# A dense layer with Mish on one core: the first load of x in two halves, one weight slab on another queue, one filler matmul fewer

## The chip, the core and the metric

The kernel runs on one core of a Trainium2 chip. The core's engines run side by side and meet at semaphores: TensorE (matmuls into the accumulators, PSUM), VectorE, ScalarE, GpSimd, and SyncE, which here only issues DMAs. A DMA is issued from an engine's queue (here SyncE's or ScalarE's); its data is moved by the core's 16 DMA engines, and a semaphore tells of its landing. The metric is the time of one execution in microseconds (us) on the device.

## The reference

All inputs are bf16. With x of 2048 tokens by 512, w1 of 512 by 1792 and w2 of 1792 by 512:

```python
h = jnp.einsum("bsd,df->bsf", x, w1) + b1
sp = jnp.log1p(jnp.exp(-jnp.abs(h))) + jnp.where(h > 0, h, jnp.zeros_like(h))
act = h * jnp.tanh(sp)
return jnp.einsum("bsf,fd->bsd", act, w2)
```

`act` is the Mish function of `h`. Two matrix products with a function between them; nearly all arithmetic is TensorE's.

## The kernel before, in words

The tokens stand in 16 tiles of 128 and in four blocks of 512 (`BLOCKS`). D = 512 is cut into four slices of 128, called k 0 to 3; F = 1792 into 14 slices f. For each block the first product (`mm1_step`, line 189) takes, for each f, four matmuls over k, with a slice of w1 as the weights and x transposed (`xT`, feature by token) as the moving operand, into one of the PSUM banks. ScalarE applies Mish with b1 as the bias (line 172) into `a_sb`. The second product (`mm2_step`, line 212) takes 14 matmuls over f for a tile of 128 tokens, then ScalarE copies the result out and SyncE stores it. A small part of tile 3 (448 columns of one f) is computed on VectorE instead (line 233), along the whole run.

The change sits in the prologue, the stretch before the first real matmul. Its parts, in order:

- Lines 113 and 6: TensorE runs fillers, matmuls on constants whose results nobody reads: five of 512 columns and two of 256 (`WARM`). They are there so that the array is at work before data has come. `t_fill[2]` is the third of them.
- Lines 115 to 118: ScalarE loads its function table, waits for a memset of VectorE (`t_bz`), and issues two loads of w1: k 0 and k 2, each for the first 8 slices f (`OPEN`), 128 partitions of 2 KB, 256 KB in all.
- Line 119: SyncE issues the load of x tiles 0 and 1 in their natural order, 128 partitions of 2 KB (`x_nat`; partition p holds the tokens 2p and 2p+1), 256 KB. Line 120: it issues k 1 of w1, 256 KB. Line 121: it waits for the third filler. Line 122: it issues a transposing load of tiles 2 and 3 straight into `xT`; then come k 3, b1, the rest of w1 (slices 8 to 13), and w2. All of these stand in SyncE's queue one behind the other.
- Lines 137 to 139: GpSimd and VectorE make an identity matrix.
- `transpose_x` (line 145): TensorE waits for `x_nat` and the identity (line 147), then turns tiles 0 and 1 with 16 small matmuls against the identity, each on 64 partitions (line 156), in four groups; after each group VectorE or ScalarE copies the result from PSUM into `xT` (line 164).
- Line 293 on: the first block in an order written out by hand: k 0 for tile 0 and f 0 to 3, then for tile 1, then k 0 for f 4 to 7 on both tiles, then k 1 and k 2 on both tiles, then k 0 to 2 on tiles 2 and 3, then k 3 on all four. Each of these matmuls waits for its own slab of w1 (`t_w1`) and for its own part of `xT` (`t_cp`).

All loads issue through `load` (line 91), which gives each its own semaphore; in the profile they all stand at line 93.

Of the kernel before, what the change touches and what calls it, by code (L numbers as in the profile page):

```python
# [4 lines left out]

P = 128
SQ = 32
WARM = (512,) * 5 + (256,) * 2
BLOCKS = (512, 512, 512, 512)
LATE = 3  # L10
VF = 1
# [26 lines left out]
def bass_standalone__dense_activation_mish__prompt_kernel(  # L38
# [16 lines left out]
    x2, out2 = x[0], out[0]  # L55
# [3 lines left out]
    OPEN = 8  # L59
    N0 = BLOCKS[0] // P  # L60

    with ExitStack() as es:
        def sb(name, shape, t):
            return es.enter_context(nc.sbuf_tensor(name, shape, t))

        x_nat = sb("x_nat", [P, 2, D], BF)
# [15 lines left out]
        def sem(name):  # L82
            return es.enter_context(nc.semaphore(name))

        sp = Stream(nc.sync, None)
        pe = Stream(nc.tensor, sem("c_pe"))
# [4 lines left out]
        def load(q, dst, src, name, transpose=False):  # L91
            s = sem(name)
            (q.eng.dma_start_transpose if transpose else q.eng.dma_start)(dst, src).then_inc(s, 16)
            return (s, 16)

        def load_w1(q, ks, a, b):
            return load(q, w1_sb[:, ks, a * P:b * P], w1v[:, ks, a * P:b * P], "s_w1_%d_%d" % (ks.start, a))
# [6 lines left out]
        def load_part(q, k0, k1, a, b):  # L104
            t = load_w1(q, slice(k0, k1), a, b)
            for f in range(a, b):
                for k in range(k0, k1):
                    t_w1[k, f] = t
# [3 lines left out]
        c_m = nc.const_aps.tensor(1.0, [P, 512], BF)  # L112
        t_fill = [pe.mark(nc.tensor.matmul(ps[:, 7, 0:n], c_w, c_m[:, 0:n], start=True, stop=True)) for n in WARM]  # L113

        act.eng.preload_act_table(ACT.Mish)  # L115
        act.wait(t_bz)
        for k in (0, 2):
            load_part(act, k, k + 1, 0, OPEN)
        t_xn = load(sp, x_nat[:, :, :], x2[0:2 * P, :].rearrange("(p j) d -> p j d", p=P), "s_xn")
        load_part(sp, 1, 2, 0, OPEN)  # L120
        sp.wait(t_fill[2])
        t_x23 = load(sp, xT[:, :, 2 * P:4 * P], x2[2 * P:4 * P, :], "s_x23", True)
        load_part(sp, 3, 4, 0, OPEN)
# [15 lines left out]
        t_id = dve.mark(nc.vector.tensor_scalar(ident[:, :], diff[:, :], 0, None, ALU.is_equal))  # L139
# [4 lines left out]

        def transpose_x():

            pe.wait(t_xn, t_id)
            H = P // 2
            for b0, eng, js, ks in ((0, dve, (0,), (0,)), (2, act, (1,), (0,)), (4, dve, (0, 1), (1,)), (6, act, (0, 1), (2, 3))):
                m = len(js)  # L150
                for i, k in enumerate(ks):
                    for n, j in enumerate(js):
                        lo = (i * m + n) * H
                        for h in (0, 1):
                            g = slice(h * H, (h + 1) * H)
                            mm = nc.tensor.matmul(ps[:, b0 + h, lo:lo + H], x_nat[g, j, k * P:(k + 1) * P], ident[g, g],  # L156
                                                  start=True, stop=True)
                eng.wait(pe.mark(mm))
                for i, k in enumerate(ks):
                    dst = xT[:, k, js[0] * P:(js[-1] + 1) * P].rearrange("p (j h t) -> p j h t", j=m, h=2)  # L160
                    src = ps[:, b0:b0 + 2, i * m * H:(i + 1) * m * H].rearrange("p h (j t) -> p j h t", j=m)
                    if m == 1:
                        dst, src = dst[:, 0], src[:, 0]
                    t = eng.mark(nc.vector.tensor_copy(dst, src) if eng is dve else act.eng.activation(dst, src, ACT.Copy))  # L164
                    for j in js:
                        t_cp[j, k] = t
                free[b0] = free[b0 + 1] = [t]
# [118 lines left out]
        def spread_b1():  # L286
# [4 lines left out]
            return dve.mark(nc.vector.tensor_copy(b1_sb[:, :], b1_T[:, 0:FT]))  # L291

        transpose_x()
        t_b1c = spread_b1()
        first(range(4), (0,), (0,))
# [74 lines left out]
```

## Time and profile before

| what | value |
|---|---|
| median of 3 runs | 104.3 us (104.25 to 104.85) |
| profiled execution | 104.08 us |
| its span, first to last instruction of the program | 102.7 us |
| granted TensorE clock over the span | 1.000 |
| DMA traffic over the span | 24.76 MB, mean 241 GB/s |

How the profile is read: PE is TensorE's matmuls, PEld its weight loads, DVE VectorE, ACT ScalarE, POOL GpSimd, SP SyncE; a trailing q (SPq, ACTq) is the engine's queue, where DMAs are issued. A row of the timeline gives the start and the length in us, the engine, the line of the code, the operation, what it writes and reads, and how many were merged; in brackets stand the idle time of the engine before it and what ended that. A matmul's length in the trace includes the passage through the array, so lengths overlap; the distance between two starts tells the pace. The time to landing of a DMA counts from the start of its issue. The chain that ended last is followed back from the last instruction, at each step to whatever released it. In the view by windows, each engine has its busy time and count, and the last three columns are the granted clock, the mean busy share of the DMA engines, and the rate in GB/s of the packets that started in the window.

### The profile page before, as it was taken

The page shows a single profiled execution, that of the slowest core. Times are in us where ns is not written, and L with a number is a line of the kernel's source. Part 1 is how long each engine was busy: PE and PEld are TensorE (multiplying, and loading weights), DVE is VectorE, ACT ScalarE, POOL GpSimd, SP SyncE. Part 2 cuts the span into 40 slices and gives each one's busy share as a digit, 9 for nine tenths or more (in the row PEclk, how much of TensorE's full clock was granted, in tenths as well). Part 3 has the DMA queues.
Part 4 walks back from the last instruction along what each step waited for, and adds up shares of the span by engine and source line. Part 5 has one row for each costly group of instructions (what it writes and reads, how often), then busy time and mean ns, then how long its engine had stood idle before and what let it go on. Part 6 is the DMA issues. An engine that isn't in the chain of part 4 may idle for free.

```text
span 102.7 us, 1352 instructions
## 1 busy us (share of the span) xinstructions
PE 99.6 (97%) x518; PEld 48.7 (47%) x527; DVE 80.0 (78%) x142; ACT 48.2 (47%) x75; POOL 0.4 (0%) x5
## 2 busy tenths in 40 slices
PE   6999999999999999999999999999999999999993
PEld 2587444444444444444444444444444444444472
DVE  1203000695979599999999999999999999999972
ACT  4301999220777781022588872222277776210210
POOL 1000000000000000000000000000000000000000
PEclk9999999999999999999999999999999999999999
DMA  2999999999799999789496838497857839111103
GB/s 62 371 281 359 366 262 360 255 330 228 303 273 228 378 429 373 201 325 297 184 320 172 338 73 364 105 347 224 293 153 306 284 124 341 67 57 51 51 0 102
DMA packets 15442, 24.76 MB, mean 241 GB/s; under 512 B 8396, under 2 KB 12748, under 8 KB 13388
## 3 DMA queue, kind: packets, MB, share of 16 engines
q1 hardware_dynamic: 15004, 24.12, 72.8%
q10 hardware_dynamic: 432, 0.56, 1.5%
q8 instruction: 4, 0.07, 0.2%
q14 instruction: 2, 0.02, 0.1%
HBM read 20.71 MB, written 2.10 MB: 222 GB/s over the span
## 4 chain that ended last, share of the span: by engine, by line
PE 97%; issue 1%; DVE 0%
PE ps L189 47%; PE ps L212 47%; PE ps L113 3%; PE ps L156 1%; DVE o_sb L271 0%
## 5 line engine op out<-in xcount | busy, mean ns | idle before, releaser
L233 DVE SCALAR_TENSOR_TENSOR acc<-w_bc,a_tok,acc 128x448 f32<-128x448 bf16 x126 | 75.4, 681 | 3.0 <-DMA w_bc<-in_w_dram 3.0
L189 PE MATMUL ps<-xT,w_sb 128*128 128x512 bf16 (+2 forms) x247 | 48.8, 355 | 0.4
L212 PE MATMUL ps<-w_sb,a_sb 128*128 128x512 bf16 (+3 forms) x248 | 48.7, 354 | 0.2
L172 ACT ACTIVATE a_sb<-ps,b_sb 128x512 bf16<-128x512 f32 x56 | 37.2, 698 | 12.8 <-PE ps L189 7.6
L189 PEld LDWEIGHTS ps<-xT,w_sb 128*128 128x128 bf16 x252 | 24.2, 98 | 24.2 <-DVE xT L164 0.3
L212 PEld LDWEIGHTS ps<-w_sb,a_sb 128*128 128x128 bf16 x252 | 23.1, 98 | 25.5 <-issue 0.3
L247 ACT ACTIVATE o_sb<-ps 128x512 bf16<-128x512 f32 x14 | 8.4, 598 | 32.7 <-PE ps L212 32.7
L230 DVE TENSOR_SCALAR acc<-w_bc,a_tok 128x448 f32<-128x448 bf16 x2 | 0.8, 450 | 10.4 <-DMA w_bc<-in_w_dram 10.4
L113 PE MATMUL ps<-const-bfloat16-1.0 128*128 128x512 bf16 (+1 forms) x7 | 2.7, 563 | 0.8 <-PEq L355 0.8
L289 DVE STREAM_TRANSPOSE b_T<-b_nat 32x32 bf16<-32x32 bf16 x4 | 0.8, 202 | 3.3 <-DMA b_nat<-in_b_dram 3.2
L164 DVE CAST xT<-ps 128x128 bf16<-128x128 f32 (+1 forms) x2 | 0.6, 352 | 2.4 <-PE ps L156 2.4
L271 ACT ACTIVATE o_sb<-ps 128x320 bf16<-128x320 f32 x1 | 0.4, 438 | 4.1 <-PE ps L212 4.1
L113 PEld LDWEIGHTS ps<-const-bfloat16-1.0 128*128 128x128 bf16 x7 | 0.9, 135 | 2.1 <-issue 2.1
L164 ACT ACTIVATE xT<-ps 128x256 bf16<-128x256 f32 (+1 forms) x3 | 0.9, 347 | 1.8 <-PE ps L156 1.7
L115 ACT ACT_TABLE_LOAD x1 | 1.3, 1283 | 0.7 <-PEq L355 0.7
L271 DVE CAST o_sb<-ps 128x128 bf16<-128x128 f32 (+1 forms) x2 | 0.5, 258 | 1.1 <-PE ps L212 1.0
L110 DVE MEMSET b_nat<- 32x64 uint32 x1 | 0.1, 112 | 0.8 <-PEq L355 0.8
L243 DVE TENSOR_TENSOR o_sb<-ps,acc 128x448 bf16<-128x448 f32 x1 | 0.6, 625 | 0.1
L241 DVE TENSOR_TENSOR acc<-acc 128x448 f32<-128x448 f32 x1 | 0.6, 624 | 0.0
L156 PEld LDWEIGHTS ps<-ident,x_nat 64*128 64x128 bf16 x16 | 0.5, 123 | 0.4 <-DMA x_nat<-in_x_dram 0.4
L156 PE MATMUL ps<-ident,x_nat 64*128 64x64 bf16 x16 | 0.6, 237 | 0.0
L139 DVE TENSOR_SCALAR ident<-diff 128x128 bf16<-128x128 int32 x1 | 0.2, 227 | 0.2 <-POOL diff L137 0.2
(7 smaller groups left out, 1.0 us busy)
## 6 DMA issues: line engine op xcount, KB each, us to landing
w_bc<-in_w_dram SPq DMA_DIRECT2D x16, 1024.0 KB, 4.9
out_dram<-o_sb SPq DMA_DIRECT2D x15, 128.0 KB, 2.3
w_sb<-in_w_dram SPq DMA_DIRECT2D x1, 1792.0 KB, 11.0
w_sb<-in_w_dram SPq DMA_DIRECT2D x1, 768.0 KB, 5.8
w_sb<-in_w_dram ACTq DMA_DIRECT2D x2, 256.0 KB, 3.7
w_sb<-in_w_dram SPq DMA_DIRECT2D x2, 256.0 KB, 3.6
x_nat<-in_x_dram SPq DMA_DIRECT2D x1, 256.0 KB, 2.6
out_dram<-o_sb SPq DMA_DIRECT2D x1, 80.0 KB, 1.6
```

The lines of the kernel that those rows point to most:

```text
L113: t_fill = [pe.mark(nc.tensor.matmul(ps[:, 7, 0:n], c_w, c_m[:, 0:n], start=True, stop=True)) for n in WARM]
L115: act.eng.preload_act_table(ACT.Mish)
L156: mm = nc.tensor.matmul(ps[:, b0 + h, lo:lo + H], x_nat[g, j, k * P:(k + 1) * P], ident[g, g], start=True, stop=True)
L164: t = eng.mark(nc.vector.tensor_copy(dst, src) if eng is dve else act.eng.activation(dst, src, ACT.Copy))
L172: t = act.mark(act.eng.activation(a_sb[:, f, starts[s]:starts[s + 1]], ps[:, bank, 0:n], ACT.Mish, bias=b1_sb[:, f:f + 1]))
L189: return nc.tensor.matmul(ps[:, bank, lo:hi], w1_sb[:, k, f * P:(f + 1) * P], xT[:, k, starts[s] + lo:starts[s] + hi], start=first, stop=( ...
L212: return nc.tensor.matmul(ps[:, bank, c:hi - lo], a_sb[:, f, i * P:(i + 1) * P], w2_sb[:, f, lo + c:hi], start=(f == 0), stop=(f == FT - 1))
L230: t = dve.mark(nc.vector.tensor_scalar(o, w, col, None, ALU.mult))
L233: t = dve.mark(nc.vector.scalar_tensor_tensor(o, w, col, o, ALU.mult, ALU.add))
L247: t = [act.mark(act.eng.activation(dst, src, ACT.Copy))]
L271: t = eng.mark(nc.vector.tensor_copy(dst, src) if eng is dve else act.eng.activation(dst, src, ACT.Copy))
L289: t = dve.mark(nc.vector.transpose(b1_T[j * SQ:(j + 1) * SQ, :], b1_nat[:, j * SQ:(j + 1) * SQ]))
```

## The change

Four edits in the prologue, no other:

- `WARM` has one filler of 256 columns instead of two.
- ScalarE issues k 0, k 1 and k 2 of w1, in this order, instead of k 0 and k 2.
- SyncE issues `x_nat` as two loads of 64 partitions each (128 KB each, partitions 0 to 63 and 64 to 127), each with its own semaphore, and no longer issues k 1. The second half stands in SyncE's queue where k 1 stood, ahead of the wait for the third filler.
- The transposes wait for the identity and for both halves.

```diff
-WARM = (512,) * 5 + (256,) * 2
+WARM = (512,) * 5 + (256,)
...
-        for k in (0, 2):
+        for k in (0, 1, 2):
             load_part(act, k, k + 1, 0, OPEN)
-        t_xn = load(sp, x_nat[:, :, :], x2[0:2 * P, :].rearrange("(p j) d -> p j d", p=P), "s_xn")
-        load_part(sp, 1, 2, 0, OPEN)
+        xv = x2[0:2 * P, :].rearrange("(p j) d -> p j d", p=P)
+        t_xn = [load(sp, x_nat[h:h + P // 2, :, :], xv[h:h + P // 2, :, :], "s_xn%d" % h) for h in (0, P // 2)]
         sp.wait(t_fill[2])
         t_x23 = load(sp, xT[:, :, 2 * P:4 * P], x2[2 * P:4 * P, :], "s_x23", True)
...
-            pe.wait(t_xn, t_id)
+            pe.wait(t_id, *t_xn)
```

## The prediction, written before the changed kernel ran

> **What bounds the kernel now.** I read the page's engine totals first, then the chain of waits that ended last in order of time, then the timeline of the first 5 us, the DMA rate in windows, and the landings of the first loads. The page:
>
> ```profile
> PE 99.6 (97%) x518; PEld 48.7 (47%) x527; DVE 80.0 (78%) x142; ACT 48.2 (47%) x75; POOL 0.4 (0%) x5
> ...
> PE 97%; issue 1%; DVE 0%
> ```
>
> TensorE is both the busiest engine and nearly the whole chain. The chain in order of time shows where it could be shorter (columns: start, length, what):
>
> ```profile
> 0.73 0.04 issue
> 0.77 2.71 PE ps L113 x7
> 3.49 0.54 PE ps L156 x16
> 4.03 0.13 issue
> 4.16 5.42 PE ps L189 x52
> 9.58 0.05 issue
> 9.64 6.85 PE ps L189 x31
> ```
>
> From 4.16 us on it is one stream of matmuls without a gap worth naming, and nothing in this change touches how many there are. What the change can move is the prologue: fillers (L113), the 16 transposes (L156), their copies, and the first real matmul at 4.16 us. If that matmul moves by d and the loads behind it keep up, the end moves by d. So the question is what ended the wait ahead of the transposes and what came between them and 4.16:
>
> ```profile
> 0.74 0.40 SPq L93 DMA_DIRECT2D x_nat<-in_x_dram  x1
> ...
> 0.95 0.86 ACTq L93 DMA_DIRECT2D w_sb<-in_w_dram  x2
> ...
> 1.20 0.41 SPq L93 DMA_DIRECT2D w_sb<-in_w_dram  x1
> ...
> 2.24 1.30 SPq L93 DMA_TRANSPOSE xT<-in_x_dram  x1
> ...
> 3.42 0.45 PEld L156 LDWEIGHTS ps<-ident,x_nat 64*128 64x128 bf16 x16 [0.41 <-DMA x_nat<-in_x_dram]
> ...
> 3.70 0.62 DVE L164 CAST xT<-ps 128x128 bf16<-128x128 f32 x2 [2.38 <-PE ps L156]
> 3.75 0.98 ACT L164 ACTIVATE xT<-ps 128x128 bf16<-128x128 f32 x3 [1.73 <-PE ps L156]
> 4.13 11.87 PEld L189 LDWEIGHTS ps<-xT,w_sb 128*128 128x128 bf16 x84 [0.26 <-DVE xT L164]
> ```
>
> The transposes start at 3.42, when x_nat lands, and the first matmul follows the first copy. From landing to matmul is a fixed path: 4.16 - 3.42 = 0.74 us. The last two fillers, each in its own timeline row:
>
> ```profile
> 2.86 0.42 PE L113 MATMUL ps<-const-bfloat16-1.0 128*128 128x256 bf16 x1
> ```
> ```profile
> 3.07 0.42 PE L113 MATMUL ps<-const-bfloat16-1.0 128*128 128x256 bf16 x1
> ```
>
> They start 0.21 us apart, so the array is free again at about 3.07 + 0.21 = 3.28. The landing, not the filler, is the last to end, by about 0.1 us.
>
> **The change, part by part.** The heart of it is the order in which the DMA engines serve the first loads. Data rates (columns after the engines: granted clock, DMA share, GB/s):
>
> ```profile
> 1.20:1.60 0.40, 0.40 (x3) 0.12 (x2) 0.12 (x1) 0.40 (x1) 0.00 (x0) 1.00 0.00 0
> ```
> ```profile
> 1.60:2.00 0.40, 0.40 (x2) 0.13 (x1) 0.00 (x0) 0.40 (x1) 0.00 (x0) 1.00 0.96 113
> 2.00:2.40 0.40, 0.40 (x2) 0.15 (x1) 0.00 (x0) 0.02 (x1) 0.00 (x0) 1.00 0.49 128
> 2.40:2.80 0.40, 0.40 (x2) 0.15 (x1) 0.00 (x0) 0.00 (x0) 0.00 (x0) 1.00 1.02 384
> 2.80:3.20 0.40, 0.40 (x3) 0.15 (x1) 0.00 (x0) 0.00 (x0) 0.00 (x0) 1.00 1.02 374
> 3.20:3.60 0.40, 0.40 (x10) 0.18 (x10) 0.00 (x0) 0.00 (x0) 0.00 (x0) 1.00 1.09 410
> 3.60:4.00 0.40, 0.40 (x16) 0.27 (x11) 0.30 (x2) 0.25 (x1) 0.00 (x0) 1.00 1.00 384
> 4.00:4.40 0.40, 0.27 (x7) 0.27 (x6) 0.32 (x1) 0.36 (x3) 0.00 (x0) 1.00 1.07 389
> ```
>
> Added up, 96 KB (of 1000 bytes) have started by 2.4 us, 250 by 2.8, 400 by 3.2, 564 by 3.6, 717 by 4.0 and 873 by 4.4. Each of the first loads is 262 KB. So one load's worth is reached at 2.83 us, two at 3.50, three at 4.18. Now the landings, from the view by tile; x_nat, then k 0 of w1 alone, then k 0 and k 1 together (so the larger is k 1), then k 1 and k 2 (the larger is k 2), then the transposed load of tiles 2-3:
>
> ```profile
> DMA to landing us min/median/max: 2.6/2.6/2.6
> ```
> ```profile
> DMA to landing us min/median/max: 3.1/3.1/3.1
> ```
> ```profile
> DMA to landing us min/median/max: 3.1/3.3/3.5
> ```
> ```profile
> DMA to landing us min/median/max: 3.5/3.9/4.3
> ```
> ```profile
> DMA to landing us min/median/max: 4.3/4.3/4.3
> ```
>
> With the issue times above: x_nat at 0.74 + 2.6 = 3.34, k 0 at 0.95 + 3.1 = 4.05, k 1 at 1.20 + 3.5 = 4.70. Each is 0.51 to 0.55 us behind the moment when the bytes up to and including it had started. That is service in the order of issue, whole loads one behind the other, whichever ring they came from. Two alternatives do not fit: had SyncE's ring been emptied first, k 1 (same ring as x_nat, issued at 1.20, and x_nat's own data began about 1 us behind its issue) would have come ahead of k 0; had the rings been shared evenly, x_nat and k 0 would have landed closer together.
>
> The terms:
>
> 1. *x_nat split.* The first half goes out at 0.74, the second when SyncE is through with the first: in k 1's place, 1.20. Between them ScalarE issues k 0 at 0.95. By the order just read the engines then serve half (131 KB), k 0 (262 KB), half (131 KB). The second half is complete when two loads' worth has moved: 3.50 instead of 2.83, so x is in 0.67 us later, at 3.34 + 0.67 = 4.01. Bounds: below, the second half follows the first directly, 0 (a gain is bounded under the rivals); above, k 1 slips in as well, 4.18 - 2.83 = 1.35. I take 0.67, since k 1 is issued behind k 0 on ScalarE, at 0.95 + 0.43 = 1.38 by the two-issue row, behind 1.20.
> 2. *The path behind it* keeps its length of 0.74 plus the 0.08 from landing to the first weight load: the first matmul moves from 4.16 to 4.83. k 0 lands earlier than before, so it does not bind.
> 3. *One filler fewer*: -0.21 us of TensorE, worth nothing, because the landing is what the transposes wait for. Its cover is the landing at 4.01; the array stands idle from 3.07 to about 4.09 instead of 3.28 to 3.42.
> 4. *k 1 and k 2 of w1.* Issuing: one more DMA on ScalarE, 0.43, ending near 2.24; its first copy is at 3.75, so nothing. k 1 stays third in the order, 4.70. From 4.16 the stream takes 5.42 us for 12288 columns (8 matmuls of 128, 44 of 256), 0.44 ns a column; k 1 is wanted 2048 columns on, 0.90 us, k 2 4096 columns on, 1.81, tiles 2-3 6144 columns on, 2.71. Before, that was 5.06, 5.97 and 6.87 against landings of 4.70, 1.38 + 4.3 = 5.68, and 2.24 + 4.3 = 6.54: margins of 0.3. With a stream from 4.83 all margins grow by 0.67. k 2 is now issued 0.43 later, and could at worst let the transposed load pass it; even 0.9 us for that fits the margin. Zero, between 0 and 0.3.
> 5. *SyncE behind the halves*: the transposed load waits for the third filler, as before, and goes out at 2.24, later than the second half's issue ends (1.20 + 0.41). Nothing moves behind it.
> 6. *One more wait on TensorE* ahead of the transposes: both counts are there when the second half lands; the chain's smallest issue gaps are 0.04 to 0.05, so 0 to 0.05, and I take 0.
>
> Sum: +0.67 us. The profiled execution took 104.08 us for a span of 102.7; it becomes 103.4 and 104.75. The median of the runs shown is 0.22 above the profiled execution, so **105.0 us**.
>
> **The rivals.**
>
> *No queueing: nothing happens (0.17).* If the second half is served directly behind the first, x lands at 3.34 as before, k 0 still at 4.05, and the time is 104.3. For it: both halves are on one ring, and the order of issue was read from whole loads of equal size only. Against it: k 0's issue is 0.25 us ahead of the second half's. The Trainium skill, "DMA: Bandwidth & Descriptors", Rules for kernel authors, says of two transfers to disjoint partition halves "Don't bother", as both use the same 16 DMA engines and only serialize; by that alone the split would be this case, 104.3. No run here shows two such halves yet.
>
> *Faster (0.10).* With halves, data might begin to move earlier and x land before 3.28, where the removed filler begins to matter. From then on each 0.1 us counts, down to a landing at 3.07 (0.27 gained). But k 0 is wanted too: 4.05 against a first weight load at 4.13, so the gain ends at about 0.08, unless k 0 lands earlier as well. 104.2 at best, 104.0 with both. Against it: the rate from 2.4 us on is already level at 370 to 410 GB/s, and a split changes no byte.
>
> *Even sharing (0.05).* If the second half alternates with k 0, it is complete when 131 + 262 = 393 KB have started, at 3.18, +0.35: 104.65.
>
> *A slow TensorE clock (0.10).* The same 256-column matmul costs less in the stream than among the fillers:
>
> ```profile
> L189 PE MATMUL ps<-xT,w_sb 128*128 128x256 bf16 x44 | 5.0, 272 | 0.0
> ...
> L113 PE MATMUL ps<-const-bfloat16-1.0 128*128 128x256 bf16 x2 | 0.6, 417 | 0.0
> ```
>
> By starts it is 0.21 us a piece in the fillers against 0.11 (256 columns of 0.44 ns) from 4.16 on, although the granted clock reads 1.00 in both. Somewhere in 3.3 to 4.16, some 3 us into steady work, the array doubled its pace. Here an idle hole of about 1 us opens ahead of the transposes. If the count starts anew at 4.09, full pace comes about 3.2 us later, at 7.3, and the 2.5 us of stream from 4.83 run at half pace and lose 1.25: 105.0 + 1.25 = 106.2. It decides if the hole counts as idle at all; against it, 2.3 us of fillers still stand ahead of it. The Trainium skill, "TensorE: Matmul & The Clock Gate", Part 1, has the pace rise after a busy window of about 3.4 us, in free-running windows; by that the trace's 3 us agree, and what a hole of 1 us does no run here shows.
>
> **How the numbers follow.** Service in order of issue 0.58 (105.0, own range 104.7 to 105.4 from terms 1, 4 and 6 and the spread of the runs); unchanged 0.17; faster 0.10; even sharing 0.05; slow clock 0.10. The range 104.15 to 105.4 leaves out the clock case, some of the faster one and the upper bound of term 1. About 1% (1.04 us) is what a measurement can tell from no change. Only the clock case (0.10) and the upper bound of 1.35 (0.03 of the 0.58) pass it upward: 0.13. Downward nothing worked out here reaches 103.3: 0.02. Within 1%: 0.85.
>
> **What would show it.** Right: x_nat's second half lands near 4.0, k 0 ahead of it near 3.7, transposes start near 4.1, the first matmul near 4.8, and from there the stream has the same length. Wrong: transposes at 3.4 or earlier with the first matmul at or under 4.16 (halves served together); transposes near 3.7 (even sharing); 256-column matmuls in the stream that start 0.21 apart (slow clock); a gap at the first use of k 2 or tiles 2-3 (term 4).

## The result, and the profile after

The changed kernel is slower: 107.92 us in the median of 6 runs (107.39 to 108.37), against 104.38 for the kernel before, run beside it (6 runs, 104.10 to 105.13). The ratio is 1.0322, with a 95% interval from 1.0274 to 1.0370. The forecast was 105.0, in a range of 104.15 to 105.4. (Runs of a kernel that were over 1.5% longer than its fastest stand in the medians given here and below, but not in the ratios.)

The profiled execution after took 107.52 us with a span of 106.2, that is 3.44 us more than the 104.08 of the execution before. The page's totals and its chain:

```profile
PE 101.4 (96%) x517; PEld 49.8 (47%) x526; DVE 80.0 (75%) x142; ACT 48.1 (45%) x75; POOL 0.4 (0%) x5
...
PE 93%; DMA 3%; issue 1%; SPq 1%; DVE 0%
```

TensorE is busy 1.8 us longer, although it runs one matmul fewer, and a DMA now stands in the chain. The chain in order of time (start, length, what):

```profile
0.67 0.06 issue
0.73 0.57 SPq L93
1.30 0.06 issue
1.36 3.51 DMA x_nat<-in_x_dram
4.87 0.14 issue
5.01 0.61 PE ps L156 x16
5.62 0.01 issue
5.63 7.38 PE ps L189 x52
13.01 0.05 issue
13.07 6.85 PE ps L189 x31
```

Two pieces hold all of the loss. The first real matmul starts at 5.63 instead of 4.16 us: 1.47. And the first 52 recorded matmuls of the stream take 7.38 us instead of 5.42: 1.96. Together 3.43 of the 3.44. From the next piece on the lengths are those of before (6.85 and 6.85).

The first piece begins in the loads. The second half of x is issued at 1.36 and lands 3.51 us later, at 4.87; the one load before had landed at 3.34. The data rates of the changed kernel (last column GB/s):

```profile
1.60:2.00 0.40, 0.40 (x2) 0.13 (x1) 0.00 (x0) 0.40 (x1) 0.00 (x0) 1.00 0.00 0
2.00:2.40 0.40, 0.40 (x2) 0.15 (x1) 0.00 (x0) 0.01 (x1) 0.00 (x0) 1.00 0.76 148
2.40:2.80 0.40, 0.40 (x2) 0.15 (x1) 0.00 (x0) 0.00 (x0) 0.00 (x0) 1.00 0.50 149
2.80:3.20 0.40, 0.40 (x2) 0.00 (x0) 0.00 (x0) 0.00 (x0) 0.00 (x0) 1.00 1.01 353
3.20:3.60 0.40, 0.08 (x1) 0.00 (x0) 0.00 (x0) 0.00 (x0) 0.00 (x0) 1.00 1.06 405
3.60:4.00 0.40, 0.00 (x0) 0.00 (x0) 0.00 (x0) 0.00 (x0) 0.00 (x0) 1.00 1.06 369
4.00:4.40 0.40, 0.00 (x0) 0.00 (x0) 0.00 (x0) 0.00 (x0) 0.00 (x0) 1.00 1.02 251
```

Nothing moves before 2.0 us, and from 2.0 to 2.8 the rate is near 150, where before it was 113 from 1.6 on and 384 from 2.4 on. The first busy column shows the other side: TensorE is empty from 3.6 on (0.08 in the window ahead), until 5.0.

The second piece is the pace. The same 256-column matmul of the stream, first between 5.6 and 9.4 us and then between 9.8 and 13 (view of groups by shape; after the bar, busy us and the mean ns of one):

```profile
L189 PE MATMUL ps<-xT,w_sb 128*128 128x256 bf16 x14 | 3.2, 421 | 0.0
```
```profile
L189 PE MATMUL ps<-xT,w_sb 128*128 128x256 bf16 x30 | 3.6, 278 | 0.0
```

421 ns is the filler's figure in the kernel before (417), 272 the stream's. So the stream ran at half pace until some time between 9.4 and 9.8 us. The granted clock reads 1.00 throughout these windows: this change of pace is not in that column.

### The profile page after: what moved, and what is told of

Read it like the earlier page. It is cut to its first block, busy times and chain, and to the rows that moved or that the text cites. A ratio compares the mean times of both kernels' runs of the same rounds, so it can differ in the third digit from the quotient of the medians.

```text
span 106.2 us, 1351 instructions
## 1 busy us (share of the span) xinstructions
PE 101.4 (96%) x517; PEld 49.8 (47%) x526; DVE 80.0 (75%) x142; ACT 48.1 (45%) x75; POOL 0.4 (0%) x5
## 4 chain that ended last, share of the span: by engine, by line
PE 93%; DMA 3%; issue 1%; SPq 1%; DVE 0%
PE ps L189 47%; PE ps L212 45%; DMA x_nat<-in_x_dram 3%; PE ps L156 1%; SPq L93 1%; DVE o_sb L271 0%
## 5 line engine op out<-in xcount | busy, mean ns | idle before, releaser
L189 PE MATMUL ps<-xT,w_sb 128*128 128x512 bf16 (+2 forms) x247 | 50.8, 367 | 0.3
L189 PEld LDWEIGHTS ps<-xT,w_sb 128*128 128x128 bf16 x252 | 25.4, 103 | 24.8 <-DVE xT L164 0.2
```

The lines of the kernel that those rows point to most:

```text
L189: return nc.tensor.matmul(ps[:, bank, lo:hi], w1_sb[:, k, f * P:(f + 1) * P], xT[:, k, starts[s] + lo:starts[s] + hi], start=first, stop=( ...
```

## The experiments

Theory A was: the engines serve loads in the order of issue, so the second half waits behind k 0, and the hole that this opens on TensorE costs the pace. Rivals came up on the way: B, the missing filler is to blame; C, three loads in a row on ScalarE; D, a load of 64 partitions is slow by itself. All ratios are against the kernel before, run on the same chip beside it.

**One filler fewer, alone.**

```diff
-WARM = (512,) * 5 + (256,) * 2
+WARM = (512,) * 5 + (256,)
```

> The kernel before with one filler of 256 columns fewer, nothing else. Theory A (the late half of x opens a hole on TensorE, the hole costs clock): x lands at 3.4 as before, the hole grows only from 0.14 to 0.35 us, so no change: 104.3, within 0.3. Theory B (the filler itself holds the clock up, and the slow stretch is its doing): the stream begins at half pace, +1 to +2 us, 105.3 to 106.3.

Ratio 1.0018 (0.9986 to 1.0049), 104.83 against 104.64. The filler by itself costs nothing that these runs can tell; B falls. (The profiled execution, 105.24, is one of the two longest of its runs: in it k 1 landed only at 6.17 and the stream waited for it, and the matmuls before that wait ran at half pace. The median has little of this.)

**k 1 on ScalarE, alone.**

```diff
-        for k in (0, 2):
+        for k in (0, 1, 2):
...
-        load_part(sp, 1, 2, 0, OPEN)
```

> The kernel before with k 1 of w1 moved to ScalarE, between k 0 and k 2; x in one load, seven fillers. Theory A: the order of service stays x, k 0, k 1, k 2; first matmul at 4.16, 104.3 within 0.3. Theory C (three loads in a row on ScalarE delay k 0 or x by themselves): x or k 0 lands 0.3 or more later, 104.6 or more.

Ratio 1.0014 (0.9982 to 1.0046), and x was in at 3.44. C falls.

**The split, alone.** Seven fillers, k 1 behind the halves on SyncE; the two lines of the split and of the wait are as in the change.

> The kernel before with x in two halves on SyncE, k 1 behind them on SyncE, seven fillers. Theory A: second half served behind k 0, x in at 4.0 to 4.9, the first matmul 0.7 to 1.5 us later, and the clock falls as in the changed kernel: 106.5 to 108. Theory B: with the filler back the clock holds, so only the landing is paid: 105.0 to 105.8.

Ratio 1.0259 (1.0206 to 1.0312), 107.65: most of the loss. Its chain:

```profile
1.36 3.33 DMA x_nat<-in_x_dram
4.68 0.14 issue
```

x is in at 4.68. Of the three edits the split is the one that costs.

**The changed kernel without a hole.**

```diff
-WARM = (512,) * 5 + (256,)
+WARM = (512,) * 11
```

> The changed kernel with fillers of 11 x 512 columns, which end near 4.8, about when the second half of x landed. Theory A: no hole, full pace from the first matmul on, only the late landing is paid: first matmul near 5.6, 105.6 to 106.0, some 2 us under the changed kernel. If the slow stretch has another cause than the hole: 107.5 to 108 as in the changed kernel.

Ratio 1.0141 (1.0102 to 1.0180), 106.18: 1.7 us under the changed kernel's 107.92, with eleven fillers instead of six. Its stream has the pace of before from the start:

```profile
0.78 4.85 PE ps L113 x11
5.62 0.20 PE ps L156 x7
5.82 0.28 DVE xT L164
6.11 0.05 issue
6.15 12.33 PE ps L189 x84
```

12.33 us for the first block; before it was 5.42 + 0.05 + 6.85 = 12.32. The fillers ran at half pace to their end, at about 5.4, and so overran the landing (5.0) by some 0.4 us; the first matmul is at 6.15, later than expected. The slow stretch and the late landing are thus two things, and the hole is what links them.

**A hole, without a late landing.**

```diff
-WARM = (512,) * 5 + (256,) * 2
+WARM = (512,) * 3
```

> The kernel before with fillers of 3 x 512 columns only: x still lands near 3.4, but TensorE stands idle from about 2.05 to 3.42. Theory A (a hole of this size makes the count of steady work start anew at 3.42): the 256-column matmuls start 0.21 apart for 3.4 us or more after 3.42, first matmul still near 4.16, +1.3 to +2.8 us, 105.9 to 107.4. If only the late landing matters and the hole is harmless: 104.6 within 0.4.

Ratio 1.0124 (1.0067 to 1.0181), 106.03. x is in at 3.43 as before, the first matmul at 4.22, and only the stream is longer:

```profile
0.74 2.69 DMA x_nat<-in_x_dram
3.43 0.05 issue
3.47 0.61 PE ps L156 x16
4.08 0.13 issue
4.22 13.52 PE ps L189 x84
```

13.52 against 12.32: 1.2 us of half pace with x on time. (A single trace proves less than the medians, 106.03 against 104.56: with k 1 moved alone, and no hole to speak of, the first block took 12.97 us in its trace.)

**A hole half as long.**

```diff
-WARM = (512,) * 5 + (256,) * 2
+WARM = (512,) * 4 + (256,)
```

> The kernel before with fillers of 4 x 512 and 1 x 256 columns, ending near 2.7: a hole of 0.7 us, half of that with three fillers, x in one load landing at 3.4. Theory A (any hole above some 0.5 us starts the count anew): +0.9 to +1.7 us like with three fillers, 105.5 to 106.3. If a hole has to fill a larger share of the stretch that is looked at: 104.6 within 0.5, as with one filler fewer.

Ratio 1.0170 (1.0126 to 1.0214), 106.26. The timeline has x still at 3.4 and the first matmul at 4.26, which waited for k 0 (in at 4.12) and not for x; the first block takes 13.63 us:

```profile
4.26 13.63 PE ps L189 x84
```

By the starts of the matmuls TensorE was idle here from 2.65 to 3.43, 0.8 us, and with three fillers from 2.01 to 3.47, 1.5. The shorter hole is no cheaper as far as the intervals tell. With one filler fewer than before (the first experiment) the hole was 0.2 us, and cost nothing.

**w1 held back behind both halves.** The changed kernel with

```diff
-WARM = (512,) * 5 + (256,)
+WARM = (512,) * 7
...
-        act.wait(t_bz)
+        act.wait(t_bz, t_fill[1])
```

> The changed kernel with ScalarE's three loads held until the second filler (1.8 us), so that both halves of x are issued ahead of k 0; fillers of 7 x 512 columns, ending near 3.8, to leave no hole. Theory A (order of service): the second half lands at 3.4 to 3.9, near 1 us earlier than in the changed kernel, the first matmul at 4.2 to 4.7, 104.5 to 105.4. Theory D (a load of 64 partitions is itself slow): the second half lands at 4.5 or later whatever stands behind it, 105.5 or more.

Ratio 1.0275 (1.0206 to 1.0344), median 108.35, scattered from 107.35 to 112.12; the profiled execution took 109.89. In it the second half landed 3.4 us after its issue at 1.36, at 4.78, although k 0 was issued only at 1.88: theory A expected 3.4 to 3.9, and missed. This was the first sign of D, but not a clean one: the second half's issue, 0.57 us long, ended only at 1.93, and in the trace's records of single DMA packets k 0's first packet starts at 3.18 and the second half's last at 4.15, so the two were served side by side. The time itself says nothing about x: k 2, issued at 2.77 and now behind the transposed load, landed at 10.04, and the stream stood still for 2.5 us for it.

```profile
2.77 7.26 DMA w_sb<-in_w_dram
```

This trace also bears on the hole. The seven fillers kept TensorE at work until about 3.7 us, the transposes began at 4.91, and after this hole of 1.2 us the stream still began at full pace: its matmuls of 128 columns start 55 ns apart, against 107 in the changed kernel. So the length of the hole alone does not decide.

**Halves cut by token instead of by partition.** The changed kernel, same queues and order, but each load with all 128 partitions and one of the two tiles:

```diff
-        t_xn = [load(sp, x_nat[h:h + P // 2, :, :], xv[h:h + P // 2, :, :], "s_xn%d" % h) for h in (0, P // 2)]
+        t_xn = [load(sp, x_nat[:, j, :], xv[:, j, :], "s_xn%d" % j) for j in (0, 1)]
```

> The changed kernel with the halves cut the other way: each load has all 128 partitions and one of the two tiles (1 KB a partition), same queues and order of issue. Theory A: the second half is still served behind k 0, x in at 4.0 to 4.9, hole, slow stretch: 106.5 to 108. Theory D (64 partitions are the trouble): issue back to 0.40 us, second half in at 3.5 or before, 104.3 to 105.

Ratio 1.0184 (1.0137 to 1.0231), 106.52. The second half is in at 4.11, not 4.87 and not 3.5: the low end of theory A's range, and not the landing that D asked for. The pace was lost here too, 13.93 us for the first block against 12.32:

```profile
4.87 13.93 PE ps L189 x84
```

The view by tile has the issues shorter, too, here for this kernel and then for the changed one (min/median/max in ns):

```profile
L93 SPq DMA_DIRECT2D x_nat<-in_x_dram x2: 390/404/417, 0.7 to 1.2; - x2
```
```profile
L93 SPq DMA_DIRECT2D x_nat<-in_x_dram x2: 567/569/571, 0.7 to 1.4; - x2
```

So both are at work: 3.34 to 4.11 (0.77) is the place behind k 0, 4.11 to 4.87 (0.76) goes with the cut by partition, in whatever way.

**The whole of x behind k 0, no split.** Seven fillers; SyncE issues k 0 and then `x_nat` in one load, ScalarE issues k 1 and k 2 after the second filler.

```diff
-        act.wait(t_bz)
-        for k in (0, 2):
+        act.wait(t_bz, t_fill[1])
+        for k in (1, 2):
             load_part(act, k, k + 1, 0, OPEN)
+        load_part(sp, 0, 1, 0, OPEN)
         t_xn = load(sp, x_nat[:, :, :], x2[0:2 * P, :].rearrange("(p j) d -> p j d", p=P), "s_xn")
-        load_part(sp, 1, 2, 0, OPEN)
```

> No split: SyncE issues k 0, then the whole of x; ScalarE holds k 1 and k 2 until the second filler; seven fillers as before. Theory A: x is complete when two loads have moved, so it lands at 4.0 to 4.4 without any load of 64 partitions, a hole from 3.28 to then (0.8 to 1.1 us), first matmul at 4.8 to 5.2; 105.0 to 105.6 if a hole of that size leaves the clock alone, 106.3 to 107.5 if it does not. Theory D: x in at 3.4 to 3.6, 104.6.

Ratio 1.0164 (1.0094 to 1.0234), 106.65. x was issued at 1.2 and landed 2.8 us later:

```profile
DMA to landing us min/median/max: 2.8/2.8/2.8
```

That is 4.0, where the order of service puts it, with no split at all; the hole (3.28 to 3.98) then cost the pace again, the 256-column matmuls taking 324 ns in the mean. A late k 1 (in at 6.62) adds a share to this time that I did not separate.

**No w1 between the halves, both cuts.** The changed kernel with `act.wait(t_bz, t_fill[1])`, `sp.wait(t_fill[6])` ahead of the transposed load, and the seven fillers of before; first with halves of 64 partitions, then with halves by token.

> The changed kernel with ScalarE's loads held until the second filler (1.8 us), the transposed load held until the last one (3.3), and seven fillers as before: nothing is issued between the two halves of 64 partitions, and nothing for 0.5 us after them. Theory A alone (order of service): second half in at 3.4 to 3.6. Theory A with D (64 partitions cost by themselves, beside the order): issue 0.57 us, first data near 2.1 us, second half in at 3.9 to 4.8.

> The same with the halves cut by token (128 partitions of 1 KB each). Theories A and D alike: issue 0.40 us, first data near 1.75, second half in at 3.2 to 3.6, like the one load before. If splitting as such costs, whatever the cut: 3.9 or later, as in the run beside it.

The chain of the first, then of the second:

```profile
0.74 0.56 SPq L93
1.30 0.06 issue
1.36 3.83 DMA x_nat<-in_x_dram
5.18 0.14 issue
```
```profile
0.74 0.40 SPq L93
1.14 0.06 issue
1.20 2.32 DMA x_nat<-in_x_dram
3.52 0.14 issue
```

5.19 against 3.52 us, with nothing else changed in the code than the cut; the first is beyond even the 3.9 to 4.8 that A and D together expected. (The profiled execution of the first took 108.56, 1.6 us over that kernel's median, so its landing may stand on the late side; in the other kernels with halves by partition x is in at 4.68 to 5.01.) The rates where only the halves were moving, first by partition, then by token:

```profile
2.00:2.40 0.40, 0.40 (x2) 0.15 (x1) 0.00 (x0) 0.01 (x1) 0.00 (x0) 1.00 0.77 169
2.40:2.80 0.40, 0.40 (x2) 0.15 (x1) 0.00 (x0) 0.00 (x0) 0.00 (x0) 1.00 0.44 164
```
```profile
2.00:2.40 0.40, 0.40 (x2) 0.15 (x1) 0.00 (x0) 0.03 (x1) 0.00 (x0) 1.00 0.68 172
2.40:2.80 0.40, 0.40 (x2) 0.15 (x1) 0.00 (x0) 0.00 (x0) 0.00 (x0) 1.00 0.65 228
```

By token, data also moves in the window ahead (110 GB/s from 1.6 to 2.0; by partition nothing). The cut by partition is later, then, here and, with k 0 between the halves, in 4.11 against 4.68 to 5.01. The rates show what is the loads' own, as D has it: the start, with 133 KB moved by 2.8 us, against 204 KB by token.

The rest is not shown to be theirs, because then w1 comes in. The longer issues put the second half at 1.36 to 1.93, and k 0 went out at 1.88, where by token the second half was out by 1.61. In the packet records of the first, k 0 begins at 3.10 and the second half's last packet starts at 4.66, side by side on the same 16 engines; in the second, k 0 begins at 2.93 and the last packet of x starts at 3.14. So nothing stood between the halves, but k 0 was not kept clear of the second one.

The times, 106.93 (ratio 1.0199, 1.0141 to 1.0258) and 106.19 (1.0120, 1.0045 to 1.0195), are not x alone: in the second, k 0 (held) is in only at 4.85, and its chain leads through a load of w that was kept back in SyncE's queue with the rest and lands at 18.88.

**The price of the order alone.** Halves by token, k 0 between them, no hole:

```diff
-WARM = (512,) * 5 + (256,)
+WARM = (512,) * 8
```

> The changed kernel with the halves cut by token, k 0 again between them, and fillers of 8 x 512 columns that end near 4.2, when the second half lands, so that no hole opens. Theory A: this is the price of the order of service alone, first matmul 0.7 to 0.9 us later than before, 105.1 to 105.7; the 256-column matmuls reach 0.11 us by 6.5 at the latest. If the clock falls without a hole: 106.5 as with the hole.

Ratio 1.0046 (1.0008 to 1.0084), 105.14 against 104.59.

```profile
0.78 3.57 PE ps L113 x8
4.35 0.54 PE ps L156 x16
4.89 0.02 issue
4.90 5.50 PE ps L189 x52
```

The first matmul is at 4.90, 0.74 later than before, and the stream has its 5.50 us (before: 5.42). This is the case that the prediction had priced at 105.0.

None of these kernels beats the one before.

## Why the prediction was wrong, point by point

Of the 3.44 us between the two profiled executions 0.67 was forecast. Term 1 was too small by 0.80 (the first matmul moved by 1.47), and 1.96 came from the pace of TensorE, which the sum put at nothing.

**What bounds the kernel, and that only the prologue can move it: right.** The whole loss lies before 13.01 us.

**Term 1, +0.67: the mechanism right, the size off.** The engines did serve half, k 0, half: in the packet records k 0 starts its packets from 2.71 to 3.67 us and the second half from 3.45 on. Where the loads have 128 partitions, x is in at 4.11 (halves by token) or 4.0 (whole load behind k 0) against the 4.01 of the term. But the halves have 64 partitions, and the term took 262 KB as 262 KB whatever their shape: it assumed the rates and the issue time of loads of 128 partitions. Measured: 1.53 instead of 0.67, and so beyond the stated upper bound of 1.35, which let k 1 slip in but kept the same rates. A part of that bound may be in it: with the longer issue the second half went out at 1.36, beside k 1 at 1.37 and not 0.18 ahead of it, and k 1's packets start at 3.78, ahead of the last of x (3.99).

**Term 2, the fixed path: right.** From landing to first matmul 5.63 - 4.87 = 0.76, forecast 0.82.

**Term 3, the filler, "worth nothing": right by itself, wrong about its cover.** Alone it changes nothing that the runs can tell (1.0018). The term noted the idle array from 3.07 to 4.09 and put no price on it.

**Terms 4 to 6: right in the sum, in part by luck.** No wait for k 1, k 2 or tiles 2-3 appears in the changed kernel's chain; moving k 1 alone gives 1.0014. But the loads did move: k 2 landed at 2.07 + 5.2 = 7.3 us and tiles 2-3 at 2.24 + 5.9 = 8.1, 1.6 later than before. A stream at full pace from 4.83 would have wanted them at 6.64 and 7.54, so both would have been some 0.6 late (an estimate from the term's own distances); the later start and the half pace hid it.

**The rival that was right had a chance of 0.10.** The slow clock was described with its mechanism and a price of 1.25; it came, at 1.96. The step that failed is the sentence "against it, 2.3 us of fillers still stand ahead of it", which took the fillers to have counted already. A hole of 0.8 us, with 1.9 us of fillers ahead of it, is enough to lose the pace (1.0170). Where x landed as the forecast had it, with the changed kernel's six fillers (halves by token, 4.11), the pace was lost as well, for 106.52, near the 106.2 of this rival. In the changed kernel the price is larger than 1.25 because the pace came back later: 4.7 us after the restart at 5.01, not 3.2. Which holes cost the pace is not settled: one of 1.2 us with 2.9 us of fillers ahead of it did not, in the trace with w1 held back.

**The other rivals.** Nothing happens, faster, and even sharing all fell with the landing at 4.87. The Trainium skill's "Don't bother" about halves of the partitions ("DMA: Bandwidth & Descriptors", Rules for kernel authors) agrees in its advice. Read as the prediction read it, as a split that costs nothing, it does not fit the cut by partition: x was in at 4.68 to 5.19, against 3.34 in one load. For halves by token with nothing between them it nearly does: 3.52.

**What stays open.** What makes the cut by partition late is not settled. Issue takes 0.57 instead of 0.40 us in each of the five kernels that have it, nothing moves before 2.0 us in any of them, and the rate of the halves in the last of them is about 165 GB/s from 2.0 to 2.8. Sharing with the w1 loads that go out beside the second half is one candidate; a slower end is another: in the changed kernel the last packet of x ends at 4.08, 0.8 us ahead of the landing, where before it ended at 3.02, 0.3 ahead. A late first packet alone is not it: with k 1 moved alone nothing moved before 2.0 us either, and x in one load was in at 3.44. As to the cut, whether it is the number of partitions or which ones they are was not tried.

## What to carry to other kernels

In these runs a load waited for what was issued ahead of it on either queue, so splitting the one load that everything waits for lets others in between; cut by partition, the pieces came later still. While TensorE is still at half pace, an idle hole of 0.8 us can cost more than the landing that caused it, so an edit that delays the first data has to be priced with the fillers that then no longer reach it. Where two rivals share a cause, as the late landing and the slow clock did here, their chances are not independent: here the first brought the second.

## What the runs showed of the hardware that was not expected

The pace of TensorE doubles some time after steady work begins, and the delay varies. Read from the starts of the single matmuls in the traces, with a hole it came 3.3 us after the restart (three fillers), 3.6 (hole of 0.8), 3.9 (halves by token), 4.7 (the changed kernel), 5.1 (whole x behind k 0), 5.3 (split alone) and 6.2 (halves of 64 partitions, no w1 between); without a hole, or with one of 0.4 us at most, 3.0 to 4.9 after the first filler (at most 5.4 where the stream stood waiting for k 1). The Trainium skill, "TensorE: Matmul & The Clock Gate", Part 1, has free-running windows of about 3.4 us, one of which must be busy: by that, a full window would end 3.4 to 6.8 us after work begins (an estimate from its figure), which fits these numbers but for the shortest ones. How much idle time it takes to lose a window the runs do not settle: with four and a half fillers of 512 columns ahead of it a hole of 0.8 us cost the pace, with seven ahead of it one of 1.2 us did not. The delay also would explain why the kernel before scatters from 104.1 to 105.3 us in the runs beside these experiments: half of each microsecond by which the pace comes later is lost. One pair of traces agrees: with k 1 moved alone the pace came near 5.6 us and not 4.2, half of which is 0.7, and its profiled execution took 104.78 against 104.08. For the scatter as a whole this is argued, not shown.

The granted clock does not miss the half pace everywhere. In the profiled execution with w1 held back it reads 0.50 from 11.4 to 14.8 us, from 1.3 us after the stream's stall of 2.5 us had ended, and the 256-column matmuls start 0.21 us apart there. At the start of a run it read 1.00 at either pace.

A full load of 256 KB on SyncE was issued in 0.40 us, a half one of 64 partitions in 0.57: fewer partitions took longer.
